# Plain float32 output product in the first chunk of a fused attention and two-layer MoE kernel

## The chip, the cores and the metric

The kernel runs on one NeuronCore of one Trainium2 chip. The metric is the device time of one execution in microseconds (us). Three runs of the kernel before took 855.36 us in the median (854.55 to 856.16).

The core has engines that each follow their own list of instructions in order: PE (TensorE, matmuls; the load of a stationary operand is shown as PEld), DVE (VectorE), ACT (ScalarE), POOL (GpSimd) and SP, which here only issues DMAs. They wait for one another through semaphores.

## The reference

```python
# sliding-window attention, 4 x 8 heads x 576 tokens x 64, window 128, ALiBi slopes
scores = scale * q @ k.T ; scores = where(mask, scores + bias, -1e9)
attn = softmax(scores) @ v                       # -> x: 2304 tokens x 512
# gated layer, d_ff = 1536, all in float32 (weights come in as float64 bits)
y = ((x @ w_a) * (x @ w_b)) @ w_out              # 2304 x 512
# routed layer: one of 8 experts for each token, 512 -> 1024 -> 512
e = argmax(y @ w_gate + modality_bias[modality_id]); g = max softmax probability
out[t] = g[t] * relu(y[t] @ w1[e]) @ w2[e]
```

## The kernel before, in words

The 2304 tokens are 18 tiles of 128, in seven chunks of 3, 2, 2, 3, 3, 3, 2 tiles (`CH`). Tokens of one chunk go through attention (four pairs of heads, `hp`; one pair and one tile is an item) and then through the gated layer in twelve steps `j`, one for each 128 columns of d_ff: 12 products `mm_ab` with `w_a` into `ps_ab0` (L498), 12 with `w_b` into `ps_ab1`, the elementwise product `gf`, and `mm_out` (L512), which adds `gf` times a 128 x 512 piece of `w_out` onto one PSUM accumulator `acc` for each tile.

Full float32 precision is made in one of two ways. With a split: a float32 operand is written as a rounded part (`F32R`, copied by ACT) and the rest (subtracted by DVE), and three products of parts are added up. Or with a plain `F32` matmul, which needs no split. `S32 = (0, 1)` and `V32 = (0,)` list the chunks whose scores, and whose probabilities times V, are plain.

Chunk 0 is a stage of its own. Its attention (12 items) is written out by hand in order, with SK = 3 items in flight. While it runs, the weights arrive as float64 bits and DVE makes float32 of them: three bit operations for each 128 x 512 piece (`f64_ops`, L429, L433, L437), then a split (L444 on ACT, L445 on DVE). One pair (`wab_jobs(j)`, the pieces of `w_a` and `w_b` of step j) is two such pieces; the piece of `w_out` (`wo_jobs(j)`) is one. Pair 0, piece 0 of `w_out` and pair 1 are the list `conv`, taken one job at a time in the items of attention; what is left comes after it. The other pairs and pieces are converted in the steps of chunk 0 (`slot0`), which also hold the eight attention items of chunk 1. The split piece of `w_out` is stored in DRAM (`wo_d`, L481) and chunks 1 to 6 fetch it again (`wo_fetch`).

The order outside of the part written out by hand is set by a scheduler with a timeline of its own; SP's DMA issues are ordered by it too. In chunk 1 DVE also computes the routing logits of chunk 0 (`junk`, L579, 24 pieces in steps 0 to 3), and after step 2 `x2_init` writes six blocks of zero rows to DRAM.

Names of buffers: `raw`, `kk` are a pair of heads of chunk 0 (`q` and `v`; `k`), `kr`, `qr`, `vr` those of later chunks, `wraw` a pair and `wor` a piece of `w_out` in float64 bits, `f64f` the float32 in the making, `g` the split of `gf`, `u` the attention output before its transpose, `pt` the masked probabilities, `xr` the split input of the layer.

Of the kernel before, what the change touches and what calls it, by code (L numbers as in the profile page):

```python
# [21 lines left out]
def attn_moe_moe2(ctx: ExitStack, tc, q, k, v, moe_w_a, moe_w_b, moe_w_out, modality_id,  # L22
# [822 lines left out]

    def x2_init():
        zrow = m1.tile([P, DM + 1], F32, tag="x2", bufs=X2B, name="zrow")
        nc.gpsimd.memset(zrow, 0.0)
        for i in range(C0[NC - 2 if NC - 2 in RD else NC - 1], NT + 1):
            nc.sync.dma_start(out=x2d[i * P:(i + 1) * P, :], in_=zrow)  # L850
# [485 lines left out]
```

## Time and profile before

| | |
|---|---|
| median of three runs | 855.36 us |
| the profiled execution | 856.61 us, of which 854.9 us are the span from the first to the last instruction |
| PE busy | 812.0 us (95%) |
| DVE, ACT, POOL busy | 570.6, 437.7, 187.8 us |
| attention of chunk 0 up to its first `mm_ab` | 0 to 45.65 us |
| steps of chunk 0 | 45.65 to 159.38 us |
| chunk 1 | 159.38 to 223.73 us |

How to read it: the span in slices of a fortieth (21.4 us) shows where PE is below its 9 and where DVE is at it.

```profile
PE   7889877999999999999999999999999999999994
DVE  6999999896796797557955594368375544447420
```

A busy PE need not be at its peak: the ends of matmuls are modelled and neighbours overlap, so what a matmul costs in a row of them is read from the distance of two starts.

### The profile page before, as it was taken

Reading aid. Unit: us, or ns where it says so; the run is one execution under the profiler, and the core shown is the slowest. Engines: PE = TensorE matmul, PEld = TensorE weight load, DVE = VectorE, ACT = ScalarE, POOL = GpSimd, SP = SyncE. Lnnn points to the kernel's source line nnn. Section 1 sums busy time; section 2 is a strip of 40 time slices with the busy share of each in tenths; the row PEclk is TensorE's granted clock in tenths of the full one; section 3 lists DMA queues with packets and bytes.
Section 4 is the critical chain, followed back from the end, with each engine's and each line's share of the span. In section 5 each row is a group of like instructions: output and inputs, shape, how many; then the busy total and the mean of one; then the engine's idle time right before and its main releaser. Section 6 shows DMA issues by size and latency. Waiting matters only on the chain.

```text
span 854.9 us, 14384 instructions
## 1 busy us (share of the span) xinstructions
PE 812.0 (95%) x4806; PEld 740.3 (87%) x4806; DVE 570.6 (67%) x1732; ACT 437.7 (51%) x1153; POOL 187.8 (22%) x245
## 2 busy tenths in 40 slices
PE   7889877999999999999999999999999999999994
PEld 5779766889899989999999999999988998989893
DVE  6999999896796797557955594368375544447420
ACT  5756674653756766566546642232245443546420
POOL 4413214022122222221222121100033130114001
PEclk8989999999999999999999999999999999999998
DMA  9994434478876556343544244647328564549201
GB/s 268 355 405 160 132 103 142 174 233 220 192 220 193 155 152 203 111 127 95 173 142 131 69 139 137 185 148 236 98 102 303 200 196 137 169 127 303 99 32 39
DMA packets 66274, 145.50 MB, mean 170 GB/s; under 512 B 11951, under 2 KB 32079, under 8 KB 66192
## 3 DMA queue, kind: packets, MB, share of 16 engines
q1 hardware_dynamic: 62576, 134.64, 51.1%
q0 software_dynamic: 3616, 9.86, 3.3%
q8 instruction: 40, 0.66, 0.3%
q14 instruction: 42, 0.34, 0.1%
HBM read 125.63 MB, written 19.11 MB: 169 GB/s over the span
## 4 chain that ended last, share of the span: by engine, by line
PE 71%; issue 8%; DVE 7%; DMA 6%; ACT 4%; POOL 2%; SPq 1%; POOLq 0%; ACTq 0%; DVEq 0%
PE ps_ab L498 29%; PE acc L512 14%; PE ps_y L1088 8%; PE ps_h L1105 8%; PE ps_o L369 4%; PE ps_s L247 2%; DMA wraw<-in_moe_w_a 1%; PE ps_p L297 1%; DMA kr<-in_k 1%; PE ps_s L243 1%; DMA qr<-in_q 1%; POOL out L1095 1%; DMA wo<-wo_d 1%; DVE wab L445 1%; DVE f64f L433 1%
## 5 line engine op out<-in xcount | busy, mean ns | idle before, releaser
L498 PE MATMUL ps_ab<-xr,wab 128*128 128x384 f32 (+1 forms) x2016 | 339.6, 317 | 7.0 <-ACT asb L1049 1.9
L498 PEld LDWEIGHTS ps_ab<-xr,wab 128*128 128x128 f32 x2016 | 308.9, 189 | 19.1 <-ACT wab L444 4.5
L512 PE MATMUL acc<-wo,g 128*128 128x512 f32 x648 | 174.1, 399 | 4.9 <-DVE wo L445 2.0
L512 PEld LDWEIGHTS acc<-wo,g 128*128 128x128 f32 x648 | 115.5, 188 | 23.9 <-DVE wo L445 3.0
L311 POOL TENSOR_SCALAR_AFFINE_SELECT pt<-pc 128x512 fp32r<-128x512 f32 (+1 forms) x72 | 57.2, 794 | 322.8 <-DVE pc L309 215.9
L1088 PE MATMUL ps_y<-w2s,h 128*128 128x512 f32 x456 | 109.7, 394 | 0.0
L1105 PE MATMUL ps_h<-xT,w1s 128*128 128x384 f32 x576 | 104.1, 337 | 0.0
L1105 PEld LDWEIGHTS ps_h<-xT,w1s 128*128 128x128 f32 x576 | 99.7, 188 | 1.1 <-issue 0.5
L1088 PEld LDWEIGHTS ps_y<-w2s,h 128*128 128x128 f32 x456 | 84.2, 188 | 16.7
L579 DVE CUSTOM_DVE_ANT_0 junk<-x,wgt 128x512 f32<-128x512 f32 x128 | 91.5, 715 | 7.7 <-DMA wgt<-in_wgt 4.6
L271 ACT ACTIVATE p<-p,mx 128x128 f32<-128x128 f32 x144 | 56.7, 396 | 30.2 <-DVE mx L261 29.6
L1056 ACT CAST g<-gf 128x256 fp32r<-128x256 f32 (+1 forms) x72 | 33.1, 459 | 62.8 <-DVE gf L1053 61.0
L1049 ACT COPY asb<-ps_ab 128x256 f32<-128x256 f32 (+1 forms) x72 | 30.6, 425 | 65.0 <-PE ps_ab L498 64.5
L1053 DVE TENSOR_TENSOR gf<-ps_ab,asb 128x256 f32<-128x256 f32 (+1 forms) x72 | 35.0, 486 | 41.8 <-PE ps_ab L498 37.1
L369 PE MATMUL ps_o<-pt,vv 128*128 128x256 f32 x360 | 56.6, 290 | 1.7 <-POOL pt L311 1.1
L313 POOL TENSOR_SCALAR_AFFINE_SELECT pt<-pc 128x512 fp32r<-128x512 f32 (+1 forms) x72 | 57.1, 792 | 0.0
L862 DVE TENSOR_TENSOR w2s<-wr,w2s 128x1024 fp32r<-128x1024 f32 x24 | 29.4, 1226 | 39.7 <-ACT w2s L861 39.5
L369 PEld LDWEIGHTS ps_o<-pt,vv 128*128 128x128 f32 x360 | 50.0, 189 | 4.1 <-POOL pt L311 1.4
L862 DVE TENSOR_TENSOR w1s<-wr,w1s 128x1024 fp32r<-128x1024 f32 x28 | 34.3, 1225 | 24.0 <-ACT w1s L861 24.0
L1095 POOL DMA_INDIRECT out<-y,idx x19 | 22.8, 1203 | 119.9 <-ACT y L1094 118.1
L284 ACT ACTIVATE p<-p,mx 128x128 f32<-128x128 f32 x120 | 41.5, 394 | 13.0 <-DVE mx L276 12.2
L1108 ACT ACTIVATE h<-ps_h 128x384 fp32r<-128x384 f32 x48 | 23.5, 492 | 47.0 <-PE ps_h L1105 47.0
(204 smaller groups left out, 1066.0 us busy)
## 6 DMA issues: line engine op xcount, KB each, us to landing
wo<-wo_d SPq DMA_DIRECT2D x72, 512.0 KB, 3.8
wr<-in_moe_w SPq DMA_DIRECT2D x56, 512.0 KB, 4.1
wgt<-in_wgt SPq DMA_DIRECT2D x24, 512.0 KB, 4.2
wraw<-in_moe_w_a SPq DMA_DIRECT2D x12, 512.0 KB, 8.9
wraw<-in_moe_w_b SPq DMA_DIRECT2D x12, 512.0 KB, 8.2
wor<-in_moe_w_out SPq DMA_DIRECT2D x12, 512.0 KB, 4.8
wo_d<-wo SPq DMA_DIRECT2D x12, 512.0 KB, 2.8
kr<-in_k SPq DMA_DIRECT2D x24, 256.0 KB, 4.2
```

The lines of the kernel that those rows point to most:

```text
L271: nc.scalar.activation(out=it.p[:, h, :], in_=it.p[:, h, :], func=AF.Exp, bias=it.mx[:, 2 + h:3 + h], scale=-1.0, accum_out=it.mx[:, 4 + h ...
L284: nc.scalar.activation(out=it.p[:, h, :], in_=it.p[:, h, :], func=AF.Copy, scale=it.mx[:, 6 + h:7 + h])
L311: nc.gpsimd.affine_select(out=it.pt[:, :, 0], in_=pc, pattern=pat + [[-1, P]], base=0, channel_multiplier=1, compare_op=ALU.is_gt, fill=0.0)
L313: nc.gpsimd.affine_select(out=it.pt[:, :, 1], in_=pc, pattern=pat + [[1, P]], base=0, channel_multiplier=-1, compare_op=ALU.is_ge, fill=0.0)
L369: nc.tensor.matmul(it.po, lhsT=a.vv[:, t + b, r].rearrange("p h d -> p (h d)"), rhs=it.pt[:, :, b, s, :], start=(i == 0), stop=(i == 5))
L498: nc.tensor.matmul(ps[:, :n], lhsT=w[:, m, r, kk * P:(kk + 1) * P], rhs=xr[:, s, kk, :n], start=(idx == 0), stop=(idx == len(terms) - 1))
L512: nc.tensor.matmul(acc[c, t], lhsT=g[:, r, t * P:(t + 1) * P], rhs=w[:, s, :], start=(j == 0 and idx == 0), stop=(j == NJ - 1 and idx == 2))
L579: nc.vector.tensor_tensor_reduce(out=junk, in0=x2[:, 0:DM], in1=wgt[:, k], scale=1.0, scalar=0.0, op0=ALU.mult, op1=ALU.add, accum_out=lgr ...
L862: nc.vector.tensor_tensor(out=dst[:, 1], in0=srcw, in1=dst[:, 0], op=ALU.subtract)
L1053: nc.vector.tensor_tensor(out=gf[:, :n], in0=psb[:, :n], in1=asb[:, :n], op=ALU.mult)
L1088: nc.tensor.matmul(pss[t], lhsT=h[:, r, f, t * P:(t + 1) * P], rhs=W2[f // 2][:, s_, f % 2, :], start=(f == 0 and i == 0), stop=(f == 7 an ...
L1105: nc.tensor.matmul(ps, lhsT=W1[f // 2][:, r, kk, (f % 2) * P:(f % 2 + 1) * P], rhs=xT[:, s_, kk, :], start=(kk == 0 and i == 0), stop=(kk ...
```

## The change

- `mm_out` of chunk 0 is one plain float32 matmul for each tile and step (`gf` times the float32 piece `f64f`), where there were three of split parts. `gf` and the piece of `w_out` are not split in chunk 0.
- The float32 piece goes to DRAM as `wo_f` (256 KB). Chunk 1 fetches it (`wos`, two buffers), splits it (`wo_split`: a copy on ACT, a subtraction on DVE), uses it and stores the parts in `wo_d` (512 KB). Chunks 2 to 6 fetch `wo_d` as before.
- `V32 = (0, 1)`: chunk 1's probabilities times V are plain. Gone for its eight items: the scaling of the probabilities (two ACT instructions each), the subtraction L309, the split of V (L225, L226), six matmuls of 256 columns (L369). New for each: four plain matmuls of 64 columns, two scalings `u` on ACT, a transpose and a copy.
- In chunk 0 one of the two scalings `u` of an item goes from DVE to ACT.
- The loads of pairs of heads 2 and 3 come after pair 0 of the weights.
- The last eight jobs of `conv`, all of pair 1, are left for after the attention of chunk 0.
- `x2_init` writes its zero rows in chunk 3, from step 5 on, a block a step, not in chunk 1.
- Scratch tiles change places: `asb` has one buffer (it had two), `gf` and `u` of chunk 0 share the tag `g`, `f64f` of `w_out` is in the tag `wo`.

```diff
-    V32 = (0,)
+    V32 = (0, 1)
...
-            if it.a.c == 0 and EVD:
+            if it.a.c == 0 and h == 0:
                 nc.vector.tensor_scalar(out=it.o[:, h], in0=it.po[:, h, 0:D],
...
+    wo_f = dram.tile([NJ, P, DM], F32, name="wo_f")
...
+    class WoOps(list):
+        def append(self, f):
+            wo_t[self.j] = f
+            nc.sync.dma_start(out=wo_f[self.j], in_=f)
...
     def wo_jobs(j):
-        fs = []
-
-        def sp():
-            wo_t[j] = m1.tile([P, 2, DM], F32R, tag="wo", bufs=WOB, name="wo")
-            f64_split(fs[0], wo_t[j], nc.vector)
-            nc.sync.dma_start(out=wo_d[j], in_=wo_t[j].bitcast(F32))
-
-        return f64_ops(wraw.pop(("o", j)), "o", fs) + [("s", sp)]
+        return f64_ops(wraw.pop(("o", j)), "o", WoOps(j))
...
+    def wo_split(j):
+        f, w = wo_s.pop(j), wo_t[j]
+        nc.scalar.copy(out=w[:, 0], in_=f)
+        nc.vector.tensor_tensor(out=w[:, 1], in0=f, in1=w[:, 0], op=ALU.subtract)
+        nc.sync.dma_start(out=wo_d[j], in_=w.bitcast(F32))
...
         for t in range(CH[c]):
+            if c == 0:
+                nc.tensor.matmul(acc[c, t], lhsT=g[:, t * P:(t + 1) * P], rhs=w, start=(j == 0), stop=(j == NJ - 1))
+                continue
...
-        a_loads(n0 - 1)
+        a_loads(CH[0])
         qq_zero(pairs[0, 0])
         make_masks(lambda: a_preps(0))
+        wab_load(0)
+        a_loads(n0 - 1)
...
-            if g >= CVS and conv:
+            if g >= CVS and len(conv) > 8:
...
-        gt = m1.tile([P, 2, MT * P], F32R, tag="g", bufs=2, name="g")
-        nc.scalar.copy(out=gt[:, 0, :n], in_=gf[:, :n])
-        (nc.gpsimd if j in GLP else nc.vector).tensor_tensor(out=gt[:, 1, :n], in0=gf[:, :n], in1=gt[:, 0, :n], op=ALU.subtract)
...
-            if c == 1 and j == 2:
+            if c == 3 and (j == 5 or j > 5 and zr):
                 x2_init()
...
             upto('o', do_pv, g - OG)
+            if c == 1:
+                wo_split(j)
+                if j + 2 < NJ:
+                    wo_fetch(j + 2, c)
```

SP's queue at the start, in the kernel before: pairs of heads 2 and 3 (`raw_2`, `kk_2`, `raw_3`, `kk_3`), a load for chunk 2 (`kr_0`) and three small constants stand ahead of pair 0 of the weights (`wraw_191`).

```order
L156 DMA raw_2_145<-in_q 128x384
L157 DMA kk_2_146<-in_k 128x384
L158 DMA raw_2_145<-in_v 128x3x128
L156 DMA raw_3_152<-in_q 128x384
L157 DMA kk_3_153<-in_k 128x384
L158 DMA raw_3_152<-in_v 128x3x128
L170 DMA kr_0_743<-in_k 64x2x384 x2
L689 DMA wg<-in_moe_w_gate 128x4x8
L690 DMA mb<-in_moe_modality_bias 128x16
L693 DMA mid_i<-in_moe_modality_id 128x18x2
L450 DMA wraw_191<-in_moe_w_a 128x1024
```

The same place now, from behind the loads of pairs of heads 0 and 1 on:

```order
L169 DMA kr_0_733<-in_k 64x2x384 x2
L177 DMA vr_0_738<-in_v 128x3x128
L449 DMA wraw_168<-in_moe_w_a 128x1024
L449 DMA wraw_168<-in_moe_w_b 128x1024
L155 DMA raw_2_171<-in_q 128x384
L156 DMA kk_2_172<-in_k 128x384
L157 DMA raw_2_171<-in_v 128x3x128
```

Pair 0 of the weights has moved ahead of pairs of heads 2 and 3; another load for chunk 2 (`vr_0`) has come in front of it.

DVE's queue at the end of chunk 0's attention, before: jobs of pair 1 (`wraw_196`) and the split of piece 0 of `w_out` stand among the scalings `u` and the subtractions `xr` of the last items.

```order
L429 TENSOR_SCALAR f64f<-wraw_196 128x512
L341 TENSOR_SCALAR u<-ps_o,mx 128x64 x2
L437 SCALAR_TENSOR_TENSOR f64f<-wor,f64f 128x512
L433 SCALAR_TENSOR_TENSOR f64f<-wraw_196,f64f 128x512
L362 TENSOR_TENSOR xr_130<-ps_ot,xr_130 128x128
L275 TENSOR_SCALAR mx<-mx 128x2
L445 TENSOR_TENSOR wo<-f64f,wo 128x512
L276 RECIPROCAL mx<-mx 128x2
L437 SCALAR_TENSOR_TENSOR f64f<-wraw_196,f64f 128x512
L341 TENSOR_SCALAR u<-ps_o,mx 128x64 x2
L429 TENSOR_SCALAR f64f<-wraw_196 128x512
L362 TENSOR_TENSOR xr_130<-ps_ot,xr_130 128x128
```

The same place now, to the first jobs of pair 1 (`wraw_197`):

```order
L340 TENSOR_SCALAR u<-ps_o,mx 128x64
L436 SCALAR_TENSOR_TENSOR f64f<-wor,f64f 128x512
L361 TENSOR_TENSOR xr_131<-ps_ot,xr_131 128x128
L274 TENSOR_SCALAR mx<-mx 128x2
L275 RECIPROCAL mx<-mx 128x2
L340 TENSOR_SCALAR u<-ps_o,mx 128x64
L361 TENSOR_TENSOR xr_131<-ps_ot,xr_131 128x128
L340 TENSOR_SCALAR u<-ps_o,mx 128x64
L361 TENSOR_TENSOR xr_131<-ps_ot,xr_131 128x128 x2
L428 TENSOR_SCALAR f64f<-wraw_197 128x512 x2
```

All of pair 1 now stands behind the last `xr` of chunk 0, and one `u` is left for each item.

PE's queue where chunk 0 ends, now (L511 is `mm_ab`, L524 the plain product of chunk 0, L368 chunk 2's probabilities times V):

```order
L511 MATMUL ps_ab_1658<-xr_131,wab_1536 128x384
L524 MATMUL acc_899<-f64f,gf 128x512
L524 MATMUL acc_900<-f64f,gf 128x512
L524 MATMUL acc_901<-f64f,gf 128x512
L368 MATMUL ps_o<-pt,vv 128x256 x6
L524 MATMUL acc_899<-f64f,gf 128x512
L524 MATMUL acc_900<-f64f,gf 128x512
L524 MATMUL acc_901<-f64f,gf 128x512
L511 MATMUL ps_ab_1703<-xr_1673,wab_515 128x256
```

The products of the last step come ahead of chunk 1's first `mm_ab`; before, the last nine stand behind fourteen of these.

## Rows read from the trace of the kernel before

**Rows 1.** Windows; per engine busy us (instructions), then granted clock, DMA share, GB/s

```profile
45.65:159.38 113.73, 99.67 (x528) 87.69 (x529) 109.55 (x268) 66.99 (x182) 28.61 (x28) 0.98 0.52 177
159.38:223.73 64.35, 62.28 (x446) 57.24 (x446) 50.52 (x181) 35.63 (x110) 12.75 (x15) 1.00 0.79 223
...
10.00:20.00 10.00, 6.47 (x35) 5.56 (x35) 4.96 (x24) 5.14 (x18) 1.88 (x5) 0.78 1.03 275
...
40.00:50.00 10.00, 7.31 (x35) 6.74 (x35) 8.72 (x30) 2.51 (x9) 1.19 (x2) 0.66 1.03 412
...
180.00:190.00 10.00, 10.00 (x73) 9.12 (x72) 9.87 (x27) 5.86 (x17) 4.40 (x4) 1.00 0.76 225
```

**Rows 2.** PE's waits from 45.65 to 159.38: total, times, longest (us)

```profile
PE ps_p L297 <- ACT p L284: 3.2, 3, 1.6
...
PE acc L512 <- DVE wo L445: 2.0, 1, 2.0
...
PE ps_o L369 <- DVE pc L309: 0.6, 1, 0.6
```

**Rows 3.** Timeline of DVE at 16 us: start, length, instruction, idle before

```profile
16.04 0.43 DVE L429 TENSOR_SCALAR f64f<-wraw 128x512 uint32<-128x512 uint32 x1 [4.84 <-DMA wraw<-in_moe_w_a]
```

**Rows 4.** Timeline of PE in chunk 0's attention: start, length, instructions, idle before

```profile
17.00 0.45 PE L351 MATMUL ps_ot<-ident,u 128*128 128x128 f32 x1 [3.40 <-DVE sm_i L717]
17.24 1.91 PE L243 MATMUL ps_s<-kk 128*128 128x256 f32 x4
...
25.88 1.03 PE L243 MATMUL ps_s<-kk 128*128 128x256 f32 x4
26.75 0.38 PE L297 MATMUL ps_p<-ident,p 128*128 128x128 f32 x2
26.96 1.00 PE L334 MATMUL ps_o<-raw,pt 128*128 128x64 f32 x8
27.80 0.28 PE L351 MATMUL ps_ot<-ident,u 128*128 128x128 f32 x1
27.92 1.03 PE L243 MATMUL ps_s<-kk 128*128 128x256 f32 x4
...
45.55 0.45 PE L351 MATMUL ps_ot<-ident,u 128*128 128x128 f32 x1 [1.61 <-DVE u L341]
45.65 3.23 PE L498 MATMUL ps_ab<-xr,wab 128*128 128x384 f32 x9
```

**Rows 5.** DVE by line and form, 45.65 to 159.38: busy us, mean ns, idle before

```profile
L437 DVE SCALAR_TENSOR_TENSOR f64f<-wraw,f64f 128x512 uint32<-128x512 uint32 x21 | 15.0, 718 | 0.1
...
L445 DVE TENSOR_TENSOR wo<-f64f,wo 128x512 fp32r<-128x512 f32 x10 | 7.6, 755 | 0.4 <-ACT wo L444 0.3
...
L993 DVE TENSOR_TENSOR g<-gf,g 128x384 fp32r<-128x384 f32 x11 | 6.0, 547 | 0.0
...
L309 DVE TENSOR_TENSOR pc<-ps_p,pc 128x256 fp32r<-128x256 f32 x12 | 4.9, 412 | 1.5 <-ACT pc L308 1.5
...
L226 DVE TENSOR_TENSOR vv<-vr,vv 128x384 fp32r<-128x384 f32 x6 | 3.7, 619 | 0.0
```

**Rows 6.** Timeline of PE in chunk 0's steps

```profile
86.00 0.96 PE L369 MATMUL ps_o<-pt,vv 128*128 128x256 f32 x6
86.80 0.27 PE L297 MATMUL ps_p<-ident,p 128*128 128x128 f32 x1
...
153.11 4.33 PE L498 MATMUL ps_ab<-xr,wab 128*128 128x384 f32 x24
157.28 2.26 PE L512 MATMUL acc<-wo,g 128*128 128x512 f32 x9
159.38 0.40 PE L498 MATMUL ps_ab<-xr,wab 128*128 128x256 f32 x2
```

**Rows 7.** Chain of waits, 0 to 60 us: start, length, what

```profile
42.58 9.77 DMA qr<-in_q
```

**Rows 8.** Timeline of PE in chunk 1

```profile
191.61 1.17 PE L512 MATMUL acc<-wo,g 128*128 128x512 f32 x4 [1.19 <-DMA wo<-wo_d]
```

More of the change, by code (lines that the diff above doesn't have):

```diff
@@ L64, in attn_moe_moe2 @@
     QPB = 1
-    EVD = 1
     PJ = 5
@@ L691, in consts_load @@
                           in_=modality_bias.rearrange("m (o e) -> o (m e)", o=1).partition_broadcast(P))
-        mid_i = cl[0] = m1.tile([P, NT, 2], I32, tag="asb", bufs=2, name="mid_i")
+        mid_i = cl[0] = m1.tile([P, NT, 2], I32, tag="gf", bufs=1, name="mid_i")
         nc.sync.dma_start(out=mid_i.rearrange("p t w -> p (t w)").rearrange("p (t w) -> p t w", w=2),
@@ L696, in consts_ap @@
     def consts_ap():
-        cl[1] = tinit = m1.tile([P, TI * TW], I32, tag="asb", name="tinit")
+        cl[1] = tinit = m1.tile([P, TI * TW], I32, tag="asb", bufs=1, name="tinit")
         nc.gpsimd.iota(tinit, pattern=[[0, TI * TW]], base=N, channel_multiplier=1)
@@ L725, in consts_b @@
         nc.gpsimd.tensor_copy(out=mid, in_=cl[0][:, :, 0])
-        tb = m1.tile([P, NT * (E + 2)], F32, tag="asb", name="tb")
+        tb = m1.tile([P, NT * (E + 2)], F32, tag="x2T", bufs=1, name="tb")
         mm1 = tb[:, 0:2 * NT].rearrange("p (m t) -> p m t", m=2)
@@ L740, in attn_moe_moe2 @@
         if WU:
-            wz = m1.tile([P, 2 * P], BF16, tag="asb", bufs=2, name="wz")
+            wz = m1.tile([P, 2 * P], BF16, tag="asb", bufs=1, name="wz")
             nc.vector.memset(wz.bitcast(F32), 0.0)
@@ L844, in upto @@
             cur[w] += 1
+    zr = []
     def x2_init():
[L847 to L850, printed above, removed]
+        if not zr:
+            zrow = m1.tile([P, DM + 1], F32, tag="x2", bufs=X2B, name="zrow")
+            nc.gpsimd.memset(zrow, 0.0)
+            zr.extend((zrow, i) for i in range(C0[NC - 2 if NC - 2 in RD else NC - 1], NT + 1))
+        zrow, i = zr.pop(0)
+        nc.sync.dma_start(out=x2d[i * P:(i + 1) * P, :], in_=zrow)
+        return bool(zr)
     SP = [mybir.EngineType.SP]
@@ L966, in V @@
                     a_pv(live.pop(g))
-        dq(hold, "s")
-        hold.clear()
         dq(jw[:4], "d")
         psa = mm_ab(c, j, 0, None if j else 1)
-        asb = m1.tile([P, MT * P], F32, tag="asb", bufs=2, name="asb")
+        asb = m1.tile([P, MT * P], F32, tag="asb", bufs=1, name="asb")
         nc.scalar.copy(out=asb[:, :n], in_=psa[:, :n])
@@ L998, in slot0 @@
         dq(jo, "d")
+        if last:
+            wo_fetch(0, 1)
+            wo_fetch(1, 1)
         if j > 0:
@@ L1003, in slot0 @@
         a_preps(n0 + cum0(j) + PJ - 1)
-        hold.extend(jo)
-        return c, j, gt, wo_t[j]
+        return c, j, gf, wo_t[j]
     pend = None
@@ L1047, in attn_moe_moe2 @@
             psa = mm_ab(c, j, 0)
-            asb = m1.tile([P, MT * P], F32, tag="asb", bufs=2, name="asb")
+            asb = m1.tile([P, MT * P], F32, tag="asb", bufs=1, name="asb")
             nc.scalar.copy(out=asb[:, :n], in_=psa[:, :n])
@@ L1197, in s_gather @@
     def s_gather(ov):
-        idx = m1.tile([P, 1], I32, tag="asb", bufs=2, name="idx")
+        idx = m1.tile([P, 1], I32, tag="asb", bufs=1, name="idx")
         nc.sync.dma_start(out=idx, in_=tab[bass.ds(ov, P), 0:1])
```

25 lines of the change are left out of this document (16 added, 9 removed).

## The prediction, made before the changed kernel ran

> **What bounds the kernel now.** I read the slices of the span first, then windows cut at the stages, then PE's waits, then timelines. PE is the engine that ends the span, and nearly all of its lost time lies before 160 us. In the steps of chunk 0 (45.65 to 159.38 us) DVE is busy 109.55 of 113.73 us and PE 99.67 [rows 1]; the other way round in chunk 1, PE 62.28 and DVE 50.52 of 64.35. So DVE sets the pace of chunk 0's steps and PE that of the rest. PE's nine waits in these steps, 0.6 to 3.2 us each in total and some 15 us together, are mostly for conversions and splits [rows 2].
>
> What PE would need there without waits, from distances of starts: 288 `mm_ab` of 384 columns at (157.28 - 153.11) / 24 = 0.174 us are 50.1 us; 108 output products at (159.38 - 157.28) / 9 = 0.233 are 25.2 [rows 6] (nine of them stand behind chunk 1's first `mm_ab` now, so 2.1 us are added to the stage); eleven items of probabilities times V at 86.80 - 86.00 = 0.80 are 8.8 [rows 6]; seven plain score items at 26.75 - 25.88 = 0.87 are 6.1 [rows 4]; split scores and transposes come to some 5 (an estimate from the same rows). That is 95 us, in a stage of 113.7 + 2.1 = 115.8. PE loses 20.8 us.
>
> Chunk 0's attention is different. From 25.88 to 27.92 one item takes 2.04 us with PE without a break [rows 4], so there PE is the pace, and DVE matters only where PE waits for it: 4.84 us of DVE for the first weights [rows 3], which PE sees as 3.40 us idle [rows 4], and the end, where PE waits 1.61 us for the last `u` [rows 4].
>
> **The change part by part.** The sum is made against the profiled execution, 856.61 us (span 854.9 and 1.7 around it), which is 1.25 above the median of the three runs.
>
> *A. Attention of chunk 0 (0 to 45.65 us).* Ahead of the first weights stood fourteen transfers of 192 KB and three constants of 42 KB, 2,730 KB; now eight of them and `vr_0`, also 192 KB, are ahead, 1,728 KB. The difference of 1.03 MB at 275 GB/s [rows 1] is 3.7 us, so they land at 12.3 instead of 16.04, and DVE, which was there at 11.2, waits 1.1: -3.7. Behind the idle time the clock was at its lower level for part of the time (0.78 granted from 10 to 20 us [rows 1]): four score records took 1.91 instead of 1.03 [rows 4], and in proportion 0.88 x 2.04 / 0.87 = 2.1 for an item. I take -1.5 (bounds 0 and -3). Pairs of heads 2 now come behind both halves of the weights, at about 15.6 us by the same rate, near the time at which their first score would be due: +0.5 (0 to 2). At the end four jobs of pair 1 and a split leave DVE's queue in front of the last `u`; at 0.72 and 0.755 [rows 5] they are up to 3.6 us, and PE waited 1.61 for the last `u` alone. I take -2.0 (bounds -1.0 and -3.6). The `u` that goes to ACT I count as nothing, since PE is the pace in the items between. A is -6.7, between -1 and -10.
>
> *B. Steps of chunk 0.* PE: the old trace has no plain product of 512 columns. The nearest rows are plain scores of 256 columns: a matmul is two records of 0.2175 us [rows 4]. Two records of 512 columns are 0.87, against 3 x 0.233 = 0.70 for the split ones: +0.17, times 36 = +6.1. Bounds: one record in place of two would be 0.435 each, -9.5 in all; with PE's weight loads in the open, another 0.2 for each of 72 records, +20. The scores' rows hide their loads under half the columns, so I keep +6.1. Chunk 1's eight items: four plain matmuls 27.80 - 26.96 = 0.84 and a transpose 27.92 - 27.80 = 0.12 [rows 4] in place of 0.80: +1.3. PE's work becomes 95.0 + 7.4 = 102.4.
>
> DVE [rows 5]: ten splits of `w_out` (-7.6), eleven of `gf` (-6.0), eight subtractions L309 (8 x 0.412 = -3.3), three splits of V (3 x 0.619 = -1.9) go; four jobs of pair 1, up to 0.72 each and shorter for the first of a piece, come in: +2.4. 109.55 - 16.4 = 93.1. So DVE falls below PE, and PE becomes the bound of this stage: what DVE gives back is 16, but only what PE had lost can be won, less the 7.4 that it now works more. ACT loses work too (scalings, copies) and is busy only 66.99 of 113.73 [rows 1].
>
> What is late next: pair 1. All eight jobs now stand behind the last `xr`, about 5 us of DVE with the scores and `gf` of the moment among them for 7 to 8, while PE has 15 `mm_ab`, a transpose and two scores, some 4 us. A new wait of about 4 us. Of the old waits I keep 5, a third: those behind ACT's probabilities and POOL's masks are no work of DVE. The stage is 102.4 + 4 + 5 = 111.4, -4.4 against 115.8. Bounds: nothing lost but the new wait, 106.4 (-9.4); 20.8 lost as before, 123.2 (+7.4).
>
> Of the new wait the clock has to be asked. Behind 1.61 us idle and smaller gaps before it the granted clock was 0.66 from 40 to 50 us and nine `mm_ab` took 3.23 us instead of 9 x 0.174 = 1.57 [rows 1, 4]; a 4 us wait may do the same. The Trainium skill, "TensorE: Matmul & The Clock Gate", section "What's actually happening", says that the lower clock is the default and that activity lifts it, which speaks against a change that makes a new gap; by it the steps behind the gap would cost another 2 us (an estimate from the 1.7 lost on the nine), and the forecast would be 847. The old trace had its low stretch at the same place and it falls away or moves, so I add nothing.
>
> *C. Chunk 1 and later.* DVE gets twelve splits of 0.755 [rows 5], 9.1 us: 50.52 + 9.1 = 59.6 of 64.35. In the first steps it is already full (9.87 of 10 from 180 to 190 [rows 1]); six splits fall there, 4.5 us, in front of or behind `gf` and the logits of chunk 0, which can wait. I take +1.5 (bounds 0 and 4.5). The piece of `w_out` no longer comes from DRAM just in time, which cost 1.19 [rows 8]; and the zero rows leave these 64 us with their DMA share of 0.79 [rows 1]: -1.2. SP holds the store of a split and behind it the next fetch, but two buffers are ahead. One buffer for `asb` costs nothing: its reader comes twelve matmuls before the next writer. The zero rows in chunk 3, where PE is busy with some DMA share to spare, and later chunks in a slightly different order: +0.5 (-1.5 to 2.5).
>
> The sum: -6.7 - 4.4 + 0.3 + 0.5 = -10.3; 856.61 - 10.3 = 846.3 for a profiled execution, 845.0 for the median.
>
> **The rivals.**
>
> 1. *The steps give nothing back (-5.9 in all, 849.5).* PE and DVE are both about full (102 and 93 of 111), so each waits for the other in turn. For it: even with DVE as the only bound PE lost 21 us, and plain products come in blocks of 2.6 us that hold up the transposes of the items behind them. Against: DVE has some 9 us of slack which it never had.
>
> 2. *Everything comes back (837.3).* PE loses only the new wait, and A gives 9: -9.4 - 9 + 0.3 is -18.1. For it: conversions run ahead. Against: the transfers. `qr` of chunk 1's pair 2 landed at 42.58 + 9.77 = 52.35 us [rows 7], in a stretch with DMA share 1.03 at 412 GB/s [rows 1]; now 1.45 MB more stand ahead of it, 3.5 us, and ACT takes it before the copy `asb` of step 2. Step 2 cannot pass 56 us, with some 87 of the 102.4 us of PE's work to come: 143 at the earliest, 18 us before 161.5.
>
> 3. *The waits are a matter of chains, not of DVE's volume (slower: 860).* Place: the steps of chunk 0 and the first of chunk 1. Price: 20.8 us lost as before on 102.4 of work, +7.4, and all six splits in the full part of chunk 1 on the path, 4.5 for 1.5, +3; with A as forecast -10.3 + 11.8 + 3 = +4.5. It decides from about 19 us lost in the steps on. For it: the largest line of rows 2 is ACT's. Against: most of the other lines are conversions, which become fewer.
>
> 4. *It does not do what it says (855).* The load order only trades one wait for another, since pairs of heads 2 come later, and the steps give nothing: within 1.7 us of before.
>
> **How the numbers follow.** The forecast has 0.50, with its own range 841 to 849; rival 1 0.20 (849 to 853), rival 2 0.14 (834 to 841), rival 3 0.10, rival 4 0.06. About 0.2%, 1.7 us, is what a measurement of this kernel can tell from no change. Faster: 0.50 + 0.20 + 0.14 = 0.84; the same 0.06; slower 0.10. From 837 to 853 lie the forecast, rival 1 and half of rival 2 and a part of rival 4, about 0.8.
>
> **What would show it.** In the profile after: DVE's first conversion job near 12 us and PE's idle time there under 1 us; the first `mm_ab` near 39 us; plain products at 0.87 us each as two records; a wait of some 4 us for `wab` of pair 1; PE above DVE in chunk 0's steps; chunk 1's first `mm_ab` near 150 us, behind all products of chunk 0; chunk 1 near 64 us long with no wait for `wo` from DRAM. The prediction is wrong if plain products cost far more than 0.87, if PE's lost time in the steps stays near 20 us, or if chunk 1 grows by more than 4.

## The result, and the profile after

The changed kernel takes 844.26 us in the median of four runs (841.29 to 846.24), the kernel before 855.76 beside it (854.55 to 857.6): ratio 0.9861, interval 0.9824 to 0.9898. The forecast was 845.0. The profiled execution is 845.42 us, its span 843.7, so 11.2 us less than the span of before; the forecast's sum was -10.3.

The total came out, its terms did not. Cut at the first `mm_ab` of each chunk, and with the 2.1 us of products that crossed a boundary put back as in the forecast:

| stretch | before | after | difference | forecast |
|---|---|---|---|---|
| A, attention of chunk 0 | 45.65 | 41.72 | -3.9 | -6.7 |
| B, steps of chunk 0 | 115.8 | 105.6 | -10.2 | -4.4 |
| C, chunk 1 | 62.25 | 61.8 | -0.45 | +0.3 |
| chunks 2 to 6 and the end | | | +3.4 | +0.5 |

B gave 5.8 more than forecast, A 2.8 less, and the later chunks cost 2.9 more, nearly all of it in chunk 3 (96.88 before, 100.18 after). B and the later chunks lie outside the bounds that the forecast gave them (B at the least 106.4, the later chunks at the most +2.5).

The slices of the span, after: PE is below 9 only in the first, the fifteenth (chunk 3) and the last slice.

```profile
PE   8999999999999989999999999999999999999994
DVE  7789997987876866658855693377376444447320
```

Windows of the kernel after, columns as in [rows 1]: A, the steps of chunk 0, chunk 1, and three stretches at a low clock.

```profile
0.00:41.72 41.72, 36.34 (x195) 27.86 (x196) 32.68 (x157) 28.38 (x101) 19.80 (x60) 0.92 0.96 292
41.72:147.33 105.61, 104.52 (x525) 85.00 (x525) 95.72 (x243) 54.95 (x162) 19.72 (x28) 0.98 0.61 208
147.33:209.13 61.80, 60.48 (x438) 56.03 (x437) 53.53 (x183) 37.79 (x108) 11.38 (x14) 1.00 0.71 221
...
16.00:25.00 9.00, 8.46 (x33) 6.63 (x34) 7.06 (x31) 5.87 (x23) 4.71 (x12) 0.62 0.97 302
...
40.00:46.00 6.00, 5.75 (x27) 5.29 (x27) 1.88 (x9) 1.91 (x10) 0.77 (x2) 0.72 1.00 391
...
306.00:312.00 6.00, 4.82 (x19) 4.41 (x20) 5.96 (x15) 2.53 (x8) 1.92 (x2) 0.72 0.40 130
```

In the steps PE and DVE have changed places: PE 99.67 to 104.52, DVE 109.55 to 95.72 [rows 1]. All that PE waits there, over 0.2 us, is two lines of 1.1 us together, where nine lines made some 15 [rows 2]:

```profile
PE ps_p L296 <- ACT p L270: 0.6, 2, 0.4
PE ps_o L333 <- POOL pt L310: 0.5, 1, 0.5
```

Timeline of DVE after, in A and at the first job of pair 1 (start, length, instruction, idle before), against [rows 3]:

```profile
12.02 0.43 DVE L428 TENSOR_SCALAR f64f<-wraw 128x512 uint32<-128x512 uint32 x1 [1.25 <-DMA wraw<-in_moe_w_a]
...
45.50 0.29 DVE L361 TENSOR_TENSOR xr<-ps_ot,xr 128x128 fp32r<-128x128 f32 x1 [2.44 <-ACT xr L359]
45.70 1.29 DVE L428 TENSOR_SCALAR f64f<-wraw 128x512 uint32<-128x512 uint32 x3
```

The first weights come 4.0 us earlier, and pair 1 starts only when the last `xr` is through. Timeline of PE after, against [rows 4, 6]:

```profile
16.20 0.33 PE L350 MATMUL ps_ot<-ident,u 128*128 128x128 f32 x1 [0.91 <-ACT u L343]
16.87 1.65 PE L242 MATMUL ps_s<-kk 128*128 128x256 f32 x4 [0.34 <-ACT kk L206]
...
41.72 3.23 PE L511 MATMUL ps_ab<-xr,wab 128*128 128x384 f32 x9
...
54.27 2.73 PE L524 MATMUL acc<-f64f,gf 128*128 128x512 f32 x6
56.84 0.27 PE L296 MATMUL ps_p<-ident,p 128*128 128x128 f32 x1
...
145.16 2.73 PE L524 MATMUL acc<-f64f,gf 128*128 128x512 f32 x6
147.33 0.92 PE L511 MATMUL ps_ab<-xr,wab 128*128 128x256 f32 x3
```

Six records of the plain product take 56.84 - 54.27 = 2.57 us, 0.428 each and 0.857 a product, against 0.70 for three split ones. The 3.40 us of idle PE at 17 us is gone, but two smaller gaps stand in its place and the low clock behind them too; and the nine first `mm_ab` take 3.23 us as before.

What stands ahead of the two gaps, on DVE and then on ACT:

```profile
14.94 0.67 DVE L432 SCALAR_TENSOR_TENSOR f64f<-wraw,f64f 128x512 uint32<-128x512 uint32 x1
15.53 0.28 DVE L340 TENSOR_SCALAR u<-ps_o,mx 128x64 f32<-128x64 f32 x1
```

```profile
15.84 0.31 ACT L343 ACTIVATE u<-ps_o,mx 128x64 f32<-128x64 f32 x1 [1.09 <-DVE u L340]
...
16.20 1.25 ACT L206 ACTIVATE kk<-raw,qscale 64x384 f32<-64x384 f32 x2
```

The two halves of an item's `u` run one behind the other: ACT's half starts after DVE's has ended, in all twelve items, in seven of them with ACT idle until then. So the wait for ACT is a wait for DVE too, whose half stood behind a bit operation. `kk` of pair of heads 2 is next in ACT's queue, and its loads had landed by 15.0 us.

Chunk 3 holds what was not foreseen. SP, then DVE, then PE, each in its own view (SPq is SP's queue: start, time in issue, what is issued):

```profile
283.63 4.58 SPq L871 DMA_DIRECT2D x2d<-zrow  x6
...
296.49 0.54 SPq L587 DMA_DIRECT2D wgt<-in_wgt  x1
```

```profile
305.96 0.69 DVE L595 CUSTOM_DVE_ANT_0 junk<-x,wgt 128x512 f32<-128x512 f32 x1 [7.28 <-DMA wgt<-in_wgt]
...
306.57 0.55 DVE L1070 TENSOR_TENSOR gf<-ps_ab,asb 128x384 f32<-128x384 f32 x1
```

```profile
307.18 3.00 PE L511 MATMUL ps_ab<-xr,wab 128*128 128x384 f32 x10 [3.35 <-DVE gf L1070]
```

The six blocks of zero rows, meant one to a step, stand together in SP's queue between two loads of a routing weight. DVE gets the second load at 305.96, 9.5 us after its issue, where the median of the 24 such loads of this kernel is 4.6 us. DVE stands 7.28 us in front of the logits, `gf` is queued behind these, and PE waits 3.35 for it; then the clock is at 0.72 from 306 to 312.

### The profile page after: what moved, and what is told of

Its sections match the earlier page's. It is cut to its first block, busy times and chain, and to the rows that moved or that the text cites. A ratio compares the mean times of both kernels' runs of the same rounds, so it can differ in the third digit from the quotient of the medians.

```text
span 843.7 us, 14338 instructions
## 1 busy us (share of the span) xinstructions
PE 818.7 (97%) x4794; PEld 737.8 (87%) x4794; DVE 556.6 (66%) x1696; ACT 428.6 (51%) x1141; POOL 179.9 (21%) x245
## 4 chain that ended last, share of the span: by engine, by line
PE 71%; DMA 10%; issue 7%; DVE 5%; ACT 3%; SPq 2%; POOL 1%; POOLq 0%; ACTq 0%; DVEq 0%
PE ps_ab L511 31%; PE acc L528 13%; PE ps_h L1128 7%; PE ps_y L1111 7%; PE acc L524 4%; PE ps_o L368 4%; DMA wgt<-in_wgt 2%; PE ps_s L246 2%; DMA wraw<-in_moe_w_a 2%; DMA wr<-in_moe_w 2%; PE ps_p L296 1%; DMA vv<-in_v 1%; POOL out L1118 1%; DMA kk<-in_k 1%; PE ps_o L333 1%
## 5 line engine op out<-in xcount | busy, mean ns | idle before, releaser
L511 PE MATMUL ps_ab<-xr,wab 128*128 128x384 f32 (+1 forms) x2016 | 347.9, 320 | 6.1 <-DVE gf L1070 4.6
L511 PEld LDWEIGHTS ps_ab<-xr,wab 128*128 128x128 f32 x2016 | 310.8, 190 | 18.5 <-DVE gf L1070 6.3
L528 PE MATMUL acc<-wo,g 128*128 128x512 f32 x540 | 143.9, 398 | 0.0
L310 POOL TENSOR_SCALAR_AFFINE_SELECT pt<-pc 128x512 fp32r<-128x512 f32 (+1 forms) x72 | 50.8, 706 | 331.4 <-DVE pc L308 189.9
L528 PEld LDWEIGHTS acc<-wo,g 128*128 128x128 f32 x540 | 96.5, 188 | 15.3
L270 ACT ACTIVATE p<-p,mx 128x128 f32<-128x128 f32 x144 | 56.8, 396 | 31.0 <-DVE mx L260 30.4
L312 POOL TENSOR_SCALAR_AFFINE_SELECT pt<-pc 128x512 fp32r<-128x512 f32 (+1 forms) x72 | 54.9, 762 | 0.0
L283 ACT ACTIVATE p<-p,mx 128x128 f32<-128x128 f32 x104 | 36.0, 395 | 25.6 <-DVE mx L275 24.1
L368 PE MATMUL ps_o<-pt,vv 128*128 128x256 f32 x312 | 48.9, 290 | 0.0
L254 DVE COPY_PREDICATED ps_s<-upper,ps_s 128x256 f32<-128x256 uint8 x72 | 30.5, 423 | 23.2 <-PE ps_s L246 15.4
```

What stands on the lines that cost most here:

```text
L270: nc.scalar.activation(out=it.p[:, h, :], in_=it.p[:, h, :], func=AF.Exp, bias=it.mx[:, 2 + h:3 + h], scale=-1.0, accum_out=it.mx[:, 4 + h ...
L283: nc.scalar.activation(out=it.p[:, h, :], in_=it.p[:, h, :], func=AF.Copy, scale=it.mx[:, 6 + h:7 + h])
L310: nc.gpsimd.affine_select(out=it.pt[:, :, 0], in_=pc, pattern=pat + [[-1, P]], base=0, channel_multiplier=1, compare_op=ALU.is_gt, fill=0.0)
L312: nc.gpsimd.affine_select(out=it.pt[:, :, 1], in_=pc, pattern=pat + [[1, P]], base=0, channel_multiplier=-1, compare_op=ALU.is_ge, fill=0.0)
L368: nc.tensor.matmul(it.po, lhsT=a.vv[:, t + b, r].rearrange("p h d -> p (h d)"), rhs=it.pt[:, :, b, s, :], start=(i == 0), stop=(i == 5))
L511: nc.tensor.matmul(ps[:, :n], lhsT=w[:, m, r, kk * P:(kk + 1) * P], rhs=xr[:, s, kk, :n], start=(idx == 0), stop=(idx == len(terms) - 1))
```

## The experiments

Each is the changed kernel with one edit, unless it says otherwise. A is the start of the first `mm_ab`; B and C run from there to chunk 2's first `mm_ab` (they are taken together since products move across the boundary between them); chunk 3 from its first `mm_ab` to chunk 4's; all from one profiled execution, in us. Medians and ratios are of all timed runs. The kernel before was timed beside each group of runs, with medians of 855.76 to 856.78; so two medians of different groups compare to about 1 us.

An edit also moves what the scheduler orders. Up to chunk 2, the instructions of PE and DVE stand in the same order in zeros_c4j6 as in the kernel after; in pv_split PE's order differs from the 24th instruction of B on, in conv_back from the 40th, in dve_more from the 23rd. A difference between two kernels is then worth the edit and the new order together.

| kernel | A | B and C | chunk 3 | median | ratio to before (interval) |
|---|---|---|---|---|---|
| before | 45.65 | 178.1 | 96.9 | 855.76 | |
| after | 41.72 | 167.4 | 100.2 | 844.26 | 0.9861 (0.9824 to 0.9898) |
| double_tile0 | 41.59 | 177.9 | 97.9 | 852.56 | 0.9938 (0.9917 to 0.9959) |
| dve_more | 40.74 | 171.0 | 97.7 | 847.26 | 0.9895 (0.9871 to 0.9920) |
| product_split | 42.28 | 182.3 | 99.1 | 858.08 | 1.0014 (0.9999 to 1.0030) |
| pv_split | 41.61 | 178.9 | 98.8 | 857.95 | 1.0010 (0.9989 to 1.0031) |
| conv_back | 41.83 | 166.2 | 98.1 | 842.88 | 0.9834 (0.9814 to 0.9854) |
| pv_split_conv | 44.94 | 164.5 | 97.2 | 842.45 | 0.9829 (0.9807 to 0.9851) |
| product_split_conv | 43.18 | 180.3 | 97.9 | 856.17 | 0.9996 (0.9985 to 1.0007) |
| loads_back | 46.87 | 167.8 | 96.8 | 847.30 | 0.9889 (0.9867 to 0.9912) |
| u_dve | 37.71 | 168.7 | 97.0 | 839.07 | 0.9788 (0.9770 to 0.9806) |
| zeros_c4j6 | 40.26 | 166.8 | 95.9 | 839.05 | 0.9790 (0.9772 to 0.9809) |
| both | 38.24 | 171.6 | 95.6 | 839.96 | 0.9799 (0.9778 to 0.9819) |
| all_three | 39.88 | 166.1 | 95.3 | 839.84 | 0.9801 (0.9782 to 0.9820) |

**What bounds chunk 0's steps.** double_tile0 gives PE twelve more products:

```diff
-                nc.tensor.matmul(acc[c, t], lhsT=..., rhs=w, start=(j == 0), stop=(j == NJ - 1))
+                for r in range(2 if t == 0 else 1):
+                    nc.tensor.matmul(acc[c, t], lhsT=..., rhs=w, ...)
```

> The changed kernel with chunk 0's plain product of tile 0 issued twice in each step (its accumulator is doubled, so the values after it are not the reference's; 12 more matmuls of two records, 12 x 0.857 = 10.3 us of PE). Theory (the steps of chunk 0 are now bound by PE, 104.5 of 105.6 us busy): the steps grow by 9 to 11 us, from 105.6 to about 116, and the run by the same. Rival (they are still paced by DVE's conversions and by chains, PE only looks busy): less than half, 0 to 5 us.

Twelve products at 0.857 are 10.3 us; B and C grew by 10.5, as the theory said, and the median by 8.3 (chunk 3 was 2.3 shorter in the profiled execution). PE's time is on the path one for one, so PE is the bound.

dve_more gives DVE one more bit operation for each piece of `w_out`:

```diff
+            if key == "o":
+                nc.vector.scalar_tensor_tensor(out=st[0], in0=rv[:, :, 0], scalar=29, in1=st[0], ...)
```

> The changed kernel with the last bit operation of each piece of w_out done twice on DVE (the value is the same), 11 more instructions of 0.6 us in the steps of chunk 0, 6.6 us in all. Theory (DVE has 95.7 busy of 105.6 us there, so it has room for them): the steps grow by 0 to 2 us. Rival (DVE still sets the pace): 5 to 7 us.

Some 6.8 us of DVE (ten operations at 0.68) made B and C 3.6 longer and the median 3.0: between the two expectations. The intervals of the two ratios overlap, so the loss itself isn't certain; but PE has new waits of 2.3 us for DVE in B, the longer of them this one:

```profile
PE ps_ab L514 <- DVE gf L1008: 1.7, 1, 1.7
```

DVE is not the bound, but about half of what is added to it seems to show. "PE bounds, DVE is free" is too simple.

**Which part of the change in precision gives the time.** product_split is the kernel before with all of the change but the plain output product (so `w_out` and `gf` are split in chunk 0 as before; the new order of the first loads and the zero rows in chunk 3 are in it too):

```diff
-    V32 = (0,)
+    V32 = (0, 1)
-            if it.a.c == 0 and EVD:
+            if it.a.c == 0 and h == 0:
...
-            if g >= CVS and conv:
+            if g >= CVS and len(conv) > 8:
...
```

> The changed kernel with chunk 0's output product of three split parts as before, so gf and w_out are split in chunk 0, w_out is stored in parts and chunk 1 fetches it; all else of the change stays, but asb has its two buffers. Theory (the plain product is the part that pays, since it takes 13.6 us of splits off DVE in the steps): DVE comes to 109 us, PE falls to 98, and the steps to 112 to 116 us, 7 to 10 more than with the change; chunk 1 the same within 1. Rival (the plain product costs what it saves, and chunk 1's plain probabilities times V and the new order bring the gain): steps of 103 to 107 us.

pv_split has, of the two plain products, only the output product; chunk 1's probabilities times V are in split parts:

```diff
-    V32 = (0, 1)
+    V32 = (0,)
```

> The changed kernel with chunk 1's probabilities times V split as before (V32 = (0,)). Theory (PE saves 1.3 us, DVE, ACT and POOL get their work back, DVE 5.7 us of it, and DVE had 10 us of room): steps of chunk 0 and chunk 1 together within 2 us of the 167.4 of the changed kernel. Rival (the shorter chain from scores to V is what removes PE's waits): 5 to 10 us more.

Each took the whole gain away: 858.08 and 857.95. That is beyond every expectation: the steps of product_split are 118.0 us (112 to 116 expected), and B and C of pv_split are 11.5 above those of the kernel after (within 2 expected, 5 to 10 by the rival). Two parts of which each seems to be worth all of it can't both be. In B alone DVE's busy time is 105.1 in the one and 100.4 in the other, so the 13.7 us that pv_split lost are far more than the 4.7 that DVE got. Timeline of PE in pv_split:

```profile
45.62 2.96 PE L511 MATMUL ps_ab<-xr,wab 128*128 128x384 f32 x15
51.18 4.54 PE L524 MATMUL acc<-f64f,gf 128*128 128x512 f32 x6 [2.60 <-DVE gf L1005]
...
140.42 4.54 PE L524 MATMUL acc<-f64f,gf 128*128 128x512 f32 x6 [2.00 <-DVE gf L1005]
```

and DVE's at the first of these places:

```profile
47.08 1.88 DVE L432 SCALAR_TENSOR_TENSOR f64f<-wraw,f64f 128x512 uint32<-128x512 uint32 x3
...
49.38 1.28 DVE L436 SCALAR_TENSOR_TENSOR f64f<-wraw,f64f 128x512 uint32<-128x512 uint32 x2
50.59 0.54 DVE L1005 TENSOR_TENSOR gf<-ps_ab,asb 128x384 f32<-128x384 f32 x1
```

The products of step 0 stand in PE's queue right behind fifteen `mm_ab`, and wait for a `gf` that stands behind the jobs of pair 1 in DVE's. In the kernel after `gf` is no earlier (51.95), but PE's queue has scores and probabilities times V ahead of the products, which run at 54.27 without a wait. Behind each gap the six records take 4.54 us, not 2.73, so each of these waits costs 1.8 us more than its length. The next kernels take pair 1 out of the way, conv_back in the kernel after and the other two in pv_split and product_split:

```diff
-            if g >= CVS and len(conv) > 8:
+            if g >= CVS and conv:
```

> The changed kernel with pair 1 taken from the list in the attention of chunk 0 as before, two jobs an item from item 8 on. Theory (the late pair 1 saves DVE jobs in front of the last u but makes PE lose the start of the steps, 10 us from the first mm_ab to step 1 and 9.8 to step 2): the first mm_ab 1 to 2 us later, steps shorter by 1 to 4 us, in sum 0 to 3 us faster. Rival (the late pair 1 pays): in sum 1 to 3 us slower.

> As pv_split (chunk 1's probabilities times V in split parts, all else of the change), and the jobs of pair 1 are taken in chunk 0's attention again. pv_split lost 11.5 us in chunk 0's steps and chunk 1 for 4.7 us more of DVE in the steps and 5 more in chunk 1. Theory of places: what it cost were four waits of PE for gf on DVE, 2.0 to 2.7 us each, with the low clock behind them; the first of them, 2.60 us at 51 us, stands behind nine jobs of pair 1 in DVE's queue and goes when these are taken earlier, with the 1.8 us of slow matmuls behind it: 4 to 5 us less than pv_split, 853 to 854. Theory of volume: DVE's total is what counts, and some 3 us of jobs leave the steps: 1 to 2 us less, 856 to 857.

> As product_split (the output product of chunk 0 in split parts, all else of the change but the float32 piece of w_out), and the jobs of pair 1 are taken in chunk 0's attention again. pv_split_conv was 15.5 us faster than pv_split, so how much of what product_split lost belongs to the late pair 1? Theory of volume: the split product keeps DVE above PE (105.1 against 104.5 us of 118.0), and in product_split PE waited for wab as late as 125, 140 and 147 us (3.3, 2.5 and 1.2 us), far behind pair 1; some 3 us of jobs less and the first wait of 3.7 us at 59 us gone give 4 to 7 us: 851 to 854, and the plain product stays worth about 10. Rival, places: as with chunk 1's probabilities the loss is all the late pair 1's; then the time is that of conv_back within 2 us, 841 to 845, and neither plain product is worth anything by itself.

(The expectation of pv_split_conv counts four waits of 2.0 to 2.7 us in pv_split; by the trace they are 2.6 and 2.0 in B, 2.7 and 0.6 in C.)

Medians of the six in a table (plain and split as in the text above):

| | pair 1 after the attention | pair 1 within it |
|---|---|---|
| both plain | 844.26 (after) | 842.88 (conv_back) |
| output product plain, chunk 1's V split | 857.95 (pv_split) | 842.45 (pv_split_conv) |
| output product split, chunk 1's V plain | 858.08 (product_split) | 856.17 (product_split_conv) |

pv_split_conv is 15.5 us faster than pv_split, far more than either expectation (4 to 5, 1 to 2): the theory of places had the right sign and a third of the size. Its B and C wait for nothing longer than 1.1 us:

```profile
PE ps_ab L511 <- DVE wab L444: 1.1, 1, 1.1
PE ps_o L368 <- POOL pt L312: 0.4, 1, 0.4
```

In B and C, pv_split has PE idle for 9.8 us, pv_split_conv for 2.1; what the clock lacked to 1.00, times the stretch, is 6.8 and 1.9. These make 12.6 of the 14.4 us between the two. DVE's volume isn't the reason: from 60 to 140 us DVE is busy 79.2 of 80 us in pv_split and 79.4 in pv_split_conv. But the edit moved PE's order as well: in pv_split_conv the products of step 0 stand behind 24 more `mm_ab`, at 57.66, and don't wait.

So the plain probabilities times V of chunk 1 are worth nothing by themselves (842.45 and 842.88); they were worth 13.7 only beside the late pair 1, where waits and the low clock behind them came with the split ones. In the kernel after, the late pair 1 makes no difference that these runs can tell (844.26 and 842.88, with intervals that overlap). The plain output product is worth 13 either way, and here the theory of volume was nearer, though the early pair 1 gave product_split 1.9 and not 4 to 7. But not all of the 13 is volume. ACT in product_split_conv:

```profile
58.07 1.02 ACT L207 ACTIVATE qq<-qr,qscale 64x256 f32<-64x256 f32 x2 [7.36 <-DMA qr<-in_q]
59.12 0.37 ACT L303 COPY pc<-ps_p 128x256 f32<-128x256 f32 x1
```

DVE:

```profile
60.47 0.56 DVE L999 TENSOR_TENSOR g<-gf,g 128x384 fp32r<-128x384 f32 x1 [5.68 <-ACT g L998]
```

and PE:

```profile
59.55 2.08 PE L243 MATMUL ps_s<-kk,qq 128*128 128x256 f32 x4 [5.10 <-ACT pc L303]
```

This is the transfer of rival 2: `qr` of a pair of chunk 1, which landed at 52.35 before [rows 7], comes at 57 to 58 us with the weights ahead of it. In product_split ACT waits 5.20 us for it and PE 3.73, here 7.36 and 5.10, with the low clock behind. In the kernel after it lands as late (57.58), but ACT takes it only at 59.94, behind other work. DVE is the pace in product_split_conv (busy 77.1 of the 79.5 us from 60.47 to 140), and it stands 5.68 us itself for ACT's copy of `gf`, a copy that the plain product doesn't need; in product_split it stands 4.73, for another result of ACT. So, as an estimate, some 5 of the 13 us belong to where one ACT instruction stands, and some 8 to the work that the plain product saves; no run splits the two.

**Attention of chunk 0, and chunk 3.** loads_back has the old order of the first loads, u_dve both scalings of chunk 0 on DVE, zeros_c4j6 the zero rows together in chunk 4:

```diff
-        a_loads(CH[0])
+        a_loads(n0 - 1)
...
-        wab_load(0)
-        a_loads(n0 - 1)
```

```diff
-            if it.a.c == 0 and h == 0:
+            if it.a.c == 0:
```

```diff
-            if c == 3 and (j == 5 or j > 5 and zr):
-                x2_init()
+            if c == 4 and j == 6:
+                while x2_init():
+                    pass
```

> The changed kernel with the old order of loads (all pairs of heads of chunk 0 ahead of pair 0 of the weights). Theory (DVE and PE then stand some 4 us for the weights as before, and nothing else pays for the new order): the first mm_ab at 45 to 47 us, the run 3 to 5 us above the changed kernel. Rival (the new order only moves the wait to the second pair of heads, the stretch at half clock from 17 to 24 us being its price): 42 to 43 us.

> The changed kernel with both scalings u of an item of chunk 0 on DVE again, as before the change. Theory (in the attention of chunk 0 the u on ACT is late, PE waited 0.91 and 0.79 us for it, and DVE has room there now, 32.7 of 41.7 us): the first mm_ab comes at 39 to 41 us, 1 to 2 us earlier than with the change. Rival (DVE was what the old kernel waited for there, 1.61 us at the end, and would be again): 42 to 44 us.

> The changed kernel with the six blocks of zero rows written in step 6 of chunk 4, where no routing weights are fetched, in place of chunk 3. Theory (in chunk 3 these writes hold up the fetch of routing weights in one queue, DVE stands 7.3 us for them and PE 3.35, with a lower clock behind it): chunk 3 falls from 100.2 to 95 to 97 us, chunk 4 stays at 93, the run is 3 to 5 us below the changed kernel, near 840. Rival (chunk 3 is longer for another reason, such as the order of its attention): within 1 us of the changed kernel.

> The changed kernel with the zero rows written in chunk 4 (as in zeros_c4j6) and both scalings u of chunk 0 on DVE (as in u_dve). Theory: the two costs lie in different stages, one in chunk 0's attention (4.0 us, PE waits for u on ACT), one in chunk 3 (about 4.3 us, the zero rows ahead of a routing weight), so they add up: ratio to the kernel before about 0.979 - 0.005 = 0.974, 833 to 835 us. Rival: u_dve had a chunk 3 of 96.98 us anyway, so its gain was partly the same one, another order of chunk 3's queue; then the two together give no more than either alone, 838 to 839 us.

> As both, and the jobs of pair 1 are taken in chunk 0's attention again (as in conv_back). Theory: the late pair 1 is worth nothing once PE is the bound of chunk 0's steps; in conv_back the steps and chunk 1 were 1.2 us shorter together, so 0 to 2 us less than both. Rival: with all u of chunk 0 on DVE, its queue in the attention is full again, and the eight jobs delay u and xr at the attention's end as in the kernel before: 2 to 4 us more than both.

conv_back, pv_split_conv, product_split_conv and all_three take pair 1 in the attention; against their counterparts without it A is 0.1, 3.3, 0.9 and 1.6 longer.

loads_back: A is 46.87, 5.2 more, and the median 3.0 more, both as the theory said. The order of the loads is worth 3 to 5 us. u_dve: A is 37.71, below the 39 to 41 of the theory, and the median 5.2 less than after. PE at the same place:

```profile
15.77 0.30 PE L350 MATMUL ps_ot<-ident,u 128*128 128x128 f32 x1 [0.16 <-DVE u L340]
15.91 1.09 PE L242 MATMUL ps_s<-kk 128*128 128x256 f32 x4
```

The gap of 0.91 is 0.16, and the clock stays up. zeros_c4j6: chunk 3 is 95.9 and the median 5.2 less. But A fell by 1.5 as well, in a stretch where its instructions are those of the kernel after, with like waits. Its window and its PE there:

```profile
16.00:25.00 9.00, 7.86 (x47) 6.12 (x48) 8.17 (x38) 7.17 (x27) 5.17 (x12) 1.00 0.97 308
```

```profile
16.08 0.33 PE L350 MATMUL ps_ot<-ident,u 128*128 128x128 f32 x1 [0.84 <-ACT u L343]
16.74 1.33 PE L242 MATMUL ps_s<-kk 128*128 128x256 f32 x4 [0.33 <-ACT kk L206]
```

Gaps of 0.84 and 0.33 left the clock at 1.00 from 16 to 25 us, with 47 of PE's instructions; gaps of 0.91 and 0.34 were followed by 0.62, with 33. double_tile0, in the same order up to there, has gaps of 0.92 and 0.33 and a clock of 0.63. Whether a small gap costs clock differs between executions of the same instructions; what decides it isn't shown. Of the 4.0 us that u_dve gains in A, 1.5 came in zeros_c4j6 without its edit, with the clock up in both.

The kernel both did not add up: 839.96, near the 838 to 839 of its rival, not 833 to 835. The reason that the rival gave holds in part (u_dve's chunk 3 was 97.0, not 100.2), but its profiled execution, at 843.34 the slowest of its five (the others have 837.85 to 840.4), also lost 3 us in B, where u_dve has the same instructions in the same order. Window of both:

```profile
58.00:67.00 9.00, 7.44 (x25) 6.69 (x26) 7.19 (x20) 6.33 (x21) 2.21 (x4) 0.62 1.03 410
```

and of u_dve:

```profile
58.00:67.00 9.00, 7.91 (x45) 6.85 (x44) 8.28 (x22) 6.40 (x21) 2.23 (x4) 1.00 1.03 405
```

That is again a low stretch behind a gap, at 58.61 in both's trace, where PE had waited 1.93 for ACT. ACT had stood for the `qr` of rival 2, until 57.24; in u_dve it had it at 56.20, and PE has no gap at that place. all_three, at 839.84, can't be told from both: that is the edge of its theory (0 to 2 us less) rather than the 2 to 4 more of its rival, but the intervals of the two ratios are wider than 2 us. So four kernels between 839 and 840 are the fastest, their intervals clear of that of the kernel after; which of the two edits one makes (both `u` on DVE, zero rows in chunk 4) doesn't matter by these runs, and making both gives nothing more that can be told.

What the zero rows cost in chunk 3: the nine other variants that write them there have 96.8 to 99.1, those that write them in chunk 4 have 95.3 to 95.9. So 1 to 4 us by these, and the 100.2 of the kernel after was a bad case with its 3.35 us gap and the low clock behind it (u_dve, in the same place, has a gap of 0.6). Not all of it need be theirs: the kernel before has no zero rows there and 96.9. And the late load isn't theirs alone: DVE stands for it 4.3 us at the longest in zeros_c4j6 too, 7.3 in the kernel after, 1.8 before.

## Why the prediction was right, and where it was not

*What bounds.* Right. PE stands above DVE in chunk 0's steps (104.5 and 95.7), and twelve more products cost what they take.

*A, -6.7 forecast, -3.9 measured.* The load order did its part: first job at 12.02 against 12.3 forecast, loads_back takes 5.2 of A back. Mis-sized were two terms. The clock, -1.5, did not come: the stretch from 16 to 25 us is at 0.62, behind a gap of 0.91 us. In zeros_c4j6, where the clock stayed up, A is 40.26, a gain of 5.4. And that gap belongs to the step counted as nothing, "The `u` that goes to ACT I count as nothing, since PE is the pace in the items between": PE waits 1.7 us for `u` on ACT, whose half follows DVE's, and u_dve gives 4.0 us of A back, 1.5 of them the clock's (though PE waits 1.6 us for DVE's `u` there, in four smaller gaps). The +0.5 for pair of heads 2 did not come: its loads were there, and the 0.34 that PE waits for `kk` is ACT's queue behind `u`. The -2.0 at the end has no firm size: PE no longer waits for the last `u`, but taking pair 1 in the attention again costs A between 0.1 and 3.3.

*B, -4.4 forecast, -10.2 measured.* The work was right: products at 0.857 (forecast 0.87). The 9 us of waits (4 for pair 1, 5 of the old ones) were 1.1; with 1.7 of slow `mm_ab` at 41.72 that is 102.4 + 2.8 = 105.2 of 105.6. The new wait for pair 1 did not come, since PE's queue had scores and other products to fill the time. In pv_split it did come, 2.60 us and 1.8 of low clock behind it. So the mechanism was there, and the order that the scheduler found decided it.

That a third of the old waits would stay was the other mis-sized term, and it rests on a misreading. The old waits were not mostly for conversions and splits: by their rows those are 6.9 of the 15.2 us, and one of the nine, 1.6 for `u`, ends at 45.55 and belongs to A. Two of the largest are put down to ACT, the line of [rows 2] and this one (total, times, longest):

```profile
PE ps_s L247 <- ACT xf L375: 2.4, 2, 1.3
```

The forecast kept these because they "are no work of DVE". But they went as well: in the kernel after, ACT's probabilities cost PE 0.6 us for 3.2, `xf` none, POOL's masks 0.5 for 1.1. The longest of them shows why, in the trace of before, on DVE, ACT and PE:

```profile
122.93 1.11 DVE L433 SCALAR_TENSOR_TENSOR f64f<-wor,f64f 128x512 uint32<-128x512 uint32 x1
123.97 0.15 DVE L276 RECIPROCAL mx<-mx 128x2 f32<-128x2 f32 x1
```

```profile
124.21 0.70 ACT L284 ACTIVATE p<-p,mx 128x128 f32<-128x128 f32 x2 [0.20 <-DVE mx L276]
```

```profile
124.67 0.62 PE L297 MATMUL ps_p<-ident,p 128*128 128x128 f32 x2 [1.64 <-ACT p L284]
```

PE waited for ACT, ACT for DVE's reciprocal, and that stood behind the bit operations of a piece of `w_out`. The engine that a wait names needn't be the one that is late. One more reading: the 20.8 us that PE was to lose before are 14.1 of idle time [rows 1] and 2 of low clock; the other 4.7 PE counts as busy.

*C.* Right within 0.8: 61.8 after 62.25, and PE waits for no `w_out` from DRAM. The splits show as the forecast's +1.5: all that PE waits in C is

```profile
PE ps_ab L511 <- DVE gf L1070: 1.3, 2, 0.8
```

DVE's busy time grew by 3.0 only, not by 9.1, to 53.5: the eleven splits in C take 8.0, but six subtractions `xr` of 2.6 and smaller work have left the stage.

*Later chunks, +0.5 forecast, +3.4 measured.* Outside the bound of 2.5. "PE is busy with some DMA share to spare" was the wrong question: what counted was what stood behind the zero rows in SP's queue, and what was queued behind that on DVE. How much of the 3.4 is the zero rows' isn't settled: chunk 3 fell by 4.3 in zeros_c4j6, but by 1 to 3 in the variants that keep them.

*The clock.* The forecast added nothing for a new gap. The Trainium skill, "TensorE: Matmul & The Clock Gate", section "What's actually happening", has the low clock as the default and activity as what lifts it, and says that how many matmuls run slow before the clock rises varies between runs of one kernel. The traces agree with the first: in the kernel after the clock is at 0.50 from 18 to 24 us, where PE works without a break, and at 1.00 from 26 us on. They agree with the second, in mid-kernel: 0.62 and 1.00 behind like gaps of the same instructions. Of the four runs of the kernel after, the slowest (846.24) has a mean granted clock of 0.987 and the fastest (841.29) one of 0.994.

The errors cancelled: B 5.8 too good, A 2.8 and the later chunks 2.9 too bad. B even passed the -9.4 that rival 2 has for it; what kept the run from rival 2's 837.3 is A, where that rival has -9, and the later chunks. The bound and the direction were understood; that the total is right within 1 us is luck.

Open: why the late pair 1 costs 15.5 us in pv_split and 1.4 at most in the kernel after. In pv_split the two waits at 51 and 140 us with their slow matmuls are 8 of it, and two more waits in chunk 1 (3.3 us) come on top; but only the first of them stands behind pair 1 in DVE's queue, the rest came with another order of PE and DVE, and no run keeps the order and moves pair 1 alone. Open too is the split of the 13 us of the output product between work and the late `qr`.

## What to carry to other kernels

Taking an operand's split out of a busy VectorE can pay although the plain float32 matmul is dearer on PE; here it paid until PE was the bound. Parts of such a change aren't additive: undo them one at a time and in pairs before one is called the cause, since here one that seemed worth 13.7 us was worth nothing. Of a DMA that is moved, ask what stands behind it in its queue and who stands behind that; spare bandwidth did not tell it here. Follow a wait past the engine that it names: twice here a wait for ACT was one for DVE's queue.
